# Retention attention inside a projection stream: attention in chunk halves on 64x64 quarters of the PE array, with the state in SBUF and the transposes on the DMA engines

## The chip, the cores and the metric

The kernel runs on one core of one Trainium2 chip. The metric is the device time in microseconds (us) of one execution; lower is better. Most executions of one kernel agree closely, but some run with part of their time at a lower TensorE clock. Each execution therefore carries a state (fast or slow) and a mean granted clock, and only fast runs enter a comparison. A time of 219 us here belongs to a profiled span that is about 1.7 us shorter, because the span starts at the first instruction; times are compared with times and spans with spans.

Engine names: PE is TensorE's matmuls, DVE is VectorE, ACT is ScalarE, POOL is GpSimd, SP is SyncE. SP only moves data here: it issues loads, stores and DMA transposes, in order.

## The reference

Linear attention with a decay per head feeds a two-layer projection network. Inputs and outputs are float32; the kernel may use bf16 inside.

```python
B, H, S, D = 4, 8, 768, 64
gamma = 1.0 - 2.0 ** (-5.0 - np.arange(H))
for t in range(S):                       # state is [B, H, 64, 64]
    state = gamma * state + outer(k[:, :, t], v[:, :, t])
    y[:, :, t] = (q[:, :, t] @ state) / sqrt(D)
x = y.transpose(0, 2, 1, 3).reshape(B * S, H * D)      # 3072 x 512
h = x @ w_in                             # 512 -> 2048
out = (h * cos(h)) @ w_out               # 2048 -> 512
```

## The kernel before

Tokens are taken in chunks of 128. A *pair* `p` is one chunk of two batches; there are twelve, 0 to 5 for the first two batches and 6 to 11 for the other two. Two pairs make a *group* of 512 tokens, and there are six groups. Attention of a pair has four steps on PE: transposes of q and k (`t`; on PE for pairs 0 to 5, by DMA from pair 6 on), scores (`a`), outputs from the state and from the masked scores (`y`), and the state update. The projections are `unit_f` (w_in, four matmuls of 512 columns) and `unit_o` (w_out, likewise).

```python
PT = 6                                    # from this pair on, transposes by DMA
...
def stage_t_dma(p):                       # SP issues it
    n = p % NB
    for w, src in enumerate((qs[n], ks[n])):
        nc.sync.dma_start_transpose(
            out=qkt[n][:, w].rearrange("p b a t -> p (b a) t"),
            in_=src.rearrange("p b h d -> p (b h d)"))
...
def stage_a(p):                           # scores: 64 rows x 128 columns of the array
    ...
    nc.tensor.matmul(ap[j][:, a, :], lhsT=kt(n, b, a)[po : po + 64, :],
                     rhs=qt(n, b, a)[po : po + 64, :], tile_position=(po, 0))
...
def stage_yb(p, b):                       # outputs: 128 rows x 64 columns
    ...
    nc.tensor.matmul(yp[ts(j, 64), a, :], lhsT=stb[p % 2][:, b, a, ts(j, 64)],
                     rhs=qt(n, b, a), start=True, stop=False, skip_group_check=True)
    ...
    nc.tensor.matmul(yp[ts(j, 64), a, :], lhsT=vs[n][:, b, 2 * a + j, :],
                     rhs=am[p % 2][b][j][:, a, :], start=(c == 0), stop=True,
                     skip_group_check=True)
...
def stage_s(p, copy_st):                  # the state accumulates in a PSUM bank
    ...
    nc.tensor.matmul(st_ps[ts(j, 64), b, a, :], lhsT=ks[n][:, b, h, :],
                     rhs=vs[n][:, b, h, :], start=(c == 0 and b == 0 and a == 0),
                     stop=True, skip_group_check=True)
```

The main loop spreads the attention steps between the projections. Pairs 4 and 5 run while only the output projection of group 0 is there to cover them; pairs 6 to 11 run two to a group inside three groups that have both projections.

```python
steps = {1: "t", 2: "a", 3: "m", 6: "y"}
plan = {g: [(8 * hf + r, 2 * (g + 1) + hf, w) for hf in range(2) for r, w in steps.items()]
        for g in range(2, NG - 1)}
plan[1] = [(4, 4, "t"), (5, 4, "a"), (6, 4, "m"), (9, 4, "y"),
           (9, 5, "t"), (10, 5, "a"), (11, 5, "m"), (14, 5, "y")]
for g in range(1, NG + 1):
    for s in range(16):
        if 1 < g < NG:
            unit_f(g, s)
        unit_o(g - 1, *divmod(s, 4))
        # then whatever plan[g] has at s; at "m": stage_t_dma(p + 1);
        # at "y": SP loads q0, q1, v0 of pair p + 3, POOL's queue the other three
```

## Time and profile before

| kernel before | |
|---|---|
| time, at first | 223.2 us, median of 3 runs (219.04 to 355.21) |
| time, with the runs beside the changed kernel | 221.41 us, median of 4 runs |
| most common fast time at full clock, all batches | 219.6 us |
| profiled span | 218.3 us, clock 1.0 |
| start, until the first output matmul of group 0 | 58.1 us |
| stage of pairs 4 and 5 | 20.5 us |
| three groups with pairs 6 to 11 | 94.4 us |
| rest, projections only | 45.3 us |

The page of the profile: busy time of an engine with its share of the span and its instructions; then PE's busy share and PE's clock, in tenths, for 40 equal slices of the span; then the chain of waits (the work that ended last, followed back) by engine.

```profile
PE 206.5 (95%) x1725; PEld 114.0 (52%) x1725; DVE 113.2 (52%) x183; ACT 118.4 (54%) x187; POOL 99.0 (45%) x113
...
PE   7986999989999999999999999999999999999993
...
PEclk9999999999999999999999999999999999999999
...
PE 80%; POOL 9%; DVE 4%; ACT 4%; issue 2%; DVEq 0%; POOLq 0%; ACTq 0%
```

PE is the limit after the first tenth of the span, and its clock is full throughout. The same by stages. A row holds start and end of the stage; its length and PE's busy time; then PE's weight loads, DVE, ACT and POOL; at the end PE's clock, the DMA engines' busy share and GB/s.

```profile
0.00:58.09 58.09, 50.82 (x589) 38.65 (x590) 40.12 (x72) 39.21 (x62) 54.40 (x67) 1.00 1.00 238
58.09:78.61 20.52, 19.76 (x210) 10.77 (x208) 7.73 (x12) 11.56 (x19) 20.47 (x22) 1.00 0.84 233
78.61:172.97 94.36, 94.36 (x737) 45.86 (x736) 53.18 (x81) 51.58 (x82) 24.15 (x26) 1.00 0.56 125
172.97:218.30 45.33, 41.61 (x193) 18.70 (x191) 12.19 (x18) 16.08 (x26) 0.00 (x0) 1.00 0.14 53
```

In the three groups PE is never idle, so what attention takes from PE there is paid in full. In the stage of pairs 4 and 5 the DMA engines are 84% busy, against 56% in the groups; that will matter.

PE's timeline shows what one attention pair costs there. Columns: start, duration, engine and line, tiles, shapes, count.

```profile
82.93 1.03 PE L305 MATMUL bank_69<-w_out_sb,gt_137 128*128 128x512 bf16 x4
83.89 0.23 PE L202 MATMUL bank_68<-qkt_121 64*128 64x128 bf16 x1
...
105.89 1.03 PE L305 MATMUL bank_65<-w_out_sb,gt_137 128*128 128x512 bf16 x4
...
107.76 0.42 PE L250 MATMUL st_ps<-vs_119,ks_116 128*64 128x64 bf16 x16
```

Matmuls of 512 columns start 0.216 us apart. The distance from the last of them before an attention step to the first after it, less 0.216, is what the step costs: 0.65 us for scores and 1.36 us for outputs and state update, together 2.0 us a pair. In each, 0.1 us at the start and 0.13 to 0.15 us at the end have no matmul starting. The Trainium skill, "TensorEngine Tiling (Array Packing)", Key Properties, says that a change of tiling mode drains TensorE; these gaps agree with it. SP's timeline, where the name of the tile tells loads (`qf`, `vf`) from transposes (`qkt`):

```profile
75.38 1.49 SPq L183 DMA_TRANSPOSE qkt_121<-qs_112  x1
76.93 1.90 SPq L183 DMA_TRANSPOSE qkt_121<-ks_115  x1
78.93 0.53 SPq L110 DMA_DIRECT2D qf_0_84<-in_q_dram  x1
...
80.17 1.64 SPq L110 DMA_DIRECT2D vf_0_104<-in_v_dram  x1
```

A DMA keeps SP standing for 0.5 to 1.9 us here. Nothing on PE waits for SP itself in this kernel, only for what it has moved.

### The profile page before, as it was taken

How to read it: one execution, taken by the hardware profiler on the slowest of the kernel's cores; microseconds unless marked ns; L12 is line 12 of the kernel's file. 1: busy time of each engine (PE TensorE's matmuls, PEld its weight loads, DVE VectorE, ACT ScalarE, POOL GpSimd, SP SyncE). 2: the span in 40 equal slices, each digit the busy share in tenths (PEclk: the TensorE clock that was granted, in tenths of full speed). 3: DMA queues.
4: the chain of work that ended last, by engine and by line, in shares of the span. 5: the costliest groups of instructions: out<-in, count | busy, mean ns of one | idle time of the engine just before them, and what ended most of it. 6: DMA issues, size and time to landing. Idle time of an engine off the chain costs nothing.

```text
span 218.3 us, 4318 instructions
## 1 busy us (share of the span) xinstructions
PE 206.5 (95%) x1725; PEld 114.0 (52%) x1725; DVE 113.2 (52%) x183; ACT 118.4 (54%) x187; POOL 99.0 (45%) x113
## 2 busy tenths in 40 slices
PE   7986999989999999999999999999999999999993
PEld 2554877968756454544544544544544544444441
DVE  4486496795714516557448537547647244433000
ACT  7365857848854656556456555555534634444120
POOL 7999999959999984729042070000000000000000
PEclk9999999999999999999999999999999999999999
DMA  6999999999476999792991942613511011110212
GB/s 156 324 161 235 264 282 236 203 305 332 116 241 164 291 223 290 182 296 54 182 250 55 158 127 82 66 48 99 51 48 51 0 48 48 51 48 2 96 62 82
DMA packets 44084, 32.78 MB, mean 150 GB/s; under 512 B 32800, under 2 KB 37664, under 8 KB 44064
## 3 DMA queue, kind: packets, MB, share of 16 engines
q0 software_dynamic: 9072, 18.35, 33.4%
q1 hardware_dynamic: 34848, 14.03, 27.6%
q8 instruction: 13, 0.21, 0.4%
q10 hardware_dynamic: 144, 0.13, 0.2%
q14 instruction: 7, 0.06, 0.1%
HBM read 27.26 MB, written 6.29 MB: 154 GB/s over the span
## 4 chain that ended last, share of the span: by engine, by line
PE 80%; POOL 9%; DVE 4%; ACT 4%; issue 2%; DVEq 0%; POOLq 0%; ACTq 0%
PE bank_65 L305 10%; PE bank_63 L281 9%; PE bank_67 L305 8%; PE bank_68 L305 6%; PE bank_66 L305 6%; PE bank_64 L281 5%; PE bank_69 L281 4%; PE bank_69 L305 4%; PE bank_66 L281 4%; PE bank_67 L281 3%; PE bank_63 L292 2%; PE bank_64 L292 2%; PE bank_63 L305 2%; PE bank_64 L305 2%; POOL qs_113 L151 1%
## 5 line engine op out<-in xcount | busy, mean ns | idle before, releaser
L281 PEld LDWEIGHTS <-w_in_sb 128*128 128x128 bf16 x256 | 24.1, 98 | 28.3
L305 PEld LDWEIGHTS <-gt_137 128*128 128x128 bf16 x192 | 18.8, 98 | 22.7
L305 PEld LDWEIGHTS <-gt_136 128*128 128x128 bf16 x192 | 18.5, 98 | 21.6
L292 PEld LDWEIGHTS <-w_in_sb 128*128 128x128 bf16 x256 | 24.6, 98 | 4.0 <-issue 0.9
L305 PE MATMUL bank_67<-w_out_sb,gt_136 128*128 128x512 bf16 x64 | 16.3, 379 | 0.0
L305 PE MATMUL bank_65<-w_out_sb,gt_136 128*128 128x512 bf16 x64 | 16.1, 379 | 0.0
L281 PE MATMUL bank_63<-xt_134,w_in_sb 128*128 128x512 bf16 x48 | 12.4, 380 | 0.0
L305 PE MATMUL bank_66<-w_out_sb,gt_137 128*128 128x512 bf16 x48 | 11.8, 379 | 0.0
L305 PE MATMUL bank_68<-w_out_sb,gt_137 128*128 128x512 bf16 x48 | 11.8, 379 | 0.0
L263 ACT ACTIVATE cosb_140<-bank_63,halfpi 128x512 bf16<-128x512 f32 x10 | 6.9, 688 | 7.3 <-PE bank_63 L281 6.4
L327 PE MATMUL bank_63<-gt_137 128*128 128x512 bf16 x29 | 9.1, 470 | 1.3 <-DVE gt_137 L130 1.3
L263 ACT ACTIVATE cosb_139<-bank_63,halfpi 128x512 bf16<-128x512 f32 x9 | 6.2, 688 | 7.5 <-PE bank_63 L281 6.5
L263 ACT ACTIVATE cosb_138<-bank_63,halfpi 128x512 bf16<-128x512 f32 x8 | 5.5, 688 | 7.7 <-PE bank_63 L281 7.5
L281 PE MATMUL bank_63<-xt_135,w_in_sb 128*128 128x512 bf16 x36 | 9.3, 380 | 0.0
L281 PE MATMUL bank_64<-xt_134,w_in_sb 128*128 128x512 bf16 x32 | 8.2, 380 | 0.0
L305 PE MATMUL bank_69<-w_out_sb,gt_137 128*128 128x512 bf16 x32 | 8.2, 379 | 0.0
L305 PE MATMUL bank_65<-w_out_sb,gt_137 128*128 128x512 bf16 x32 | 8.2, 379 | 0.0
L255 DVE CAST stb_133<-st_ps 64x512 bf16<-64x512 f32 x8 | 5.5, 689 | 5.0 <-PE st_ps L250 4.8
L312 DVE COPY ob_111<-bank_68 128x256 f32<-128x256 f32 x1 | 0.4, 425 | 13.3 <-PE bank_68 L305 13.3
L263 ACT ACTIVATE cosb_140<-bank_64,halfpi 128x512 bf16<-128x512 f32 x7 | 4.8, 688 | 4.6 <-PE bank_64 L281 3.0
L281 PE MATMUL bank_69<-xt_135,w_in_sb 128*128 128x512 bf16 x28 | 7.2, 379 | 0.0
L281 PE MATMUL bank_66<-xt_135,w_in_sb 128*128 128x512 bf16 x28 | 7.2, 379 | 0.0
(399 smaller groups left out, 501.4 us busy)
## 6 DMA issues: line engine op xcount, KB each, us to landing
w_out_sb<-in_moe_w_out_dram POOLq DMA_DIRECT2D x4, 512.0 KB, 9.9
w_in_sb<-in_moe_w_in_dram POOLq DMA_DIRECT2D x3, 512.0 KB, 7.5
out_dram<-ob_108 SPq DMA_DIRECT2D x6, 256.0 KB, 2.2
out_dram<-ob_109 SPq DMA_DIRECT2D x6, 256.0 KB, 2.0
out_dram<-ob_110 SPq DMA_DIRECT2D x6, 256.0 KB, 2.1
out_dram<-ob_111 SPq DMA_DIRECT2D x5, 256.0 KB, 2.0
kf_1_89<-in_k_dram POOLq DMA_DIRECT2D x3, 256.0 KB, 5.0
vf_1_99<-in_v_dram POOLq DMA_DIRECT2D x3, 256.0 KB, 5.1
```

What stands on the lines that cost most here:

```text
L151: eng.tensor_tensor(out=qs[p % NB][:, b], in0=qf[p % PRE][b], in1=bc(gq, p % NC), op=ALU.mult)
L255: copy_st(out=stb[(p + 1) % 2][ts(j, 64), :, :, ts(j, 64)], in_=st_ps[ts(j, 64)])
L263: nc.scalar.activation(out=cb, in_=bank, func=AF.Sin, bias=halfpi)
L281: nc.tensor.matmul(bank, lhsT=w_in_sb[:, i, ts(f, 128)], rhs=xt[g % 2][:, i, :], start=(i == 0), stop=(i == KIN - 1))
L292: nc.tensor.matmul(bank[:, ts(e, 256)], lhsT=w_in_sb[:, i, ts(f + e, 128)], rhs=xt[g % 2][:, i, ts(hf, 256)], start=(i == 0 and e == 0), s ...
L305: nc.tensor.matmul(bank, lhsT=gt[g % 2][:, f, ts(j, 128)], rhs=w_out_sb[:, f, :], start=(f == 0), stop=(f == KOUT - 1))
L312: nc.vector.tensor_copy(out=o[:, ts(0, 256)], in_=bank[:, ts(0, 256)])
L327: nc.tensor.matmul(spare, lhsT=zero[:, :128], rhs=zero, start=True, stop=True, skip_group_check=True)
```

## The change

The intent is to use PE better in attention. From pair 4 on, a chunk is handled as two halves of 64 tokens. Each matmul then needs only a 64x64 quarter of the array, so that four can run at once. Scores across the two halves are not needed: the first half goes through the state. Scores, outputs and state update use the same tiling, so all attention of a step forms one block with one change of mode. The block that finishes pair `p` also does scores and state update of pair `p + 1`. The state moves from PSUM to SBUF, DVE adds to it. Pair 5's transposes go to the DMA engines too. The number of attention matmuls of a full pair rises from 64 to 128. (The prediction's 80 counts the 16 transposes too, which PE makes only for pairs 0 to 5; its estimate doesn't rest on that number.)

Two matmuls that add into one place of PSUM may now come from different quarters, so the order of the output sums is enforced: the first output sum of a block waits for a `nop` on SP, which waits for the last score matmul. It is called *the hop* below. Where a block has nothing to overlap (the last pair), PE drains instead. The core of the diff, long cuts marked:

```diff
-    PT = 6
+    PQ = 4
+    PT = 5
...
+    def block(py=None, pa=None, pu=None):
...
+        def mm(bank, col, cols, row, lhsT, rhs):
+            ...
+            return nc.tensor.matmul(bank[half(col), cols], lhsT=lhsT, rhs=rhs, start=first,
+                                    stop=True, skip_group_check=True,
+                                    tile_position=(64 * row, 64 * col))
+        # state part of py's outputs; scores of pa (last = mm(...)); state update of pu
...
+        if py is not None:
+            n = py % NB
+            hop = None
+            if pu is None:
+                nc.tensor.drain()
+            else:
+                hop = nc.sync.nop(nofuse=True)
+                tc.add_manual_dep(hop.ins, last.ins.name, SYNC, reason="sums in order")
+            for b, a in BA:
+                for j in range(2):
+                    for u in range(2):
+                        m = mm(yb[u, b], j, ts(a, 64), u, vs[n][half(u), b, 2 * a + j, :],
+                               am[py % 2][j ^ b ^ u][half(u), b, a, :])
+                        if hop is not None:
+                            tc.add_manual_dep(m.ins, hop.ins.name, SYNC, reason="sums in order")
+                            hop = None
+        # masks and state adds on DVE, copies of outputs and state on ACT
...
-    conv_q(4, nc.gpsimd)
-    conv_k(4, True)
-    conv_v(4, nc.gpsimd)
-    load(nc.gpsimd, 6, ("q0", "q1", "k0", "k1", "v0", "v1"))
+    conv_q(4, nc.vector)
+    ...
+    conv_q(5, nc.vector)
+    conv_k(5)
+    stage_t_dma(5)
+    conv_v(5, nc.gpsimd)
...
+    plan = {g: [(5, "b", 2 * g + 2), (5, "c", 2 * g + 4),
+                (13, "b", 2 * g + 3), (13, "c", 2 * g + 5)] for g in range(2, NG - 1)}
+    plan[1] = [(2, "t", 4), (3, "a", 4), (4, "c", 6), (8, "b", 4), (9, "c", 7), (14, "b", 5)]
...
+                elif what == "c":
+                    conv_q(p, nc.vector if g == 1 else nc.gpsimd)
+                    conv_k(p)
+                    stage_t_dma(p)
+                    if p == 6:
+                        load(nc.sync, 7, ("q", "v0"))
+                        load(nc.gpsimd, 7, ("k", "v1"))
+                    conv_v(p, nc.gpsimd)
+                    if p + 2 < NP:
+                        load(nc.sync, p + 2, ("q", "v0"))
+                        load(nc.gpsimd, p + 2, ("k", "v1"))
```

Step `c` prepares a pair two ahead of the block. For pair 6, in the stage of pairs 4 and 5, it puts two transposes and four loads (pairs 7 and 8) on SP in one go, ahead of the hop of pair 4's outputs in SP's order.

## The prediction

> **What bounds the kernel.** The page has PE at 95% of a 218.3 us span, and the chain of waits is 80% PE. By stages (busy time by windows): 0 to 22.5 us start-up, waiting on POOL and loads; 22.5 to 58.2 the first four pairs; 58.2 to 78.7 output matmuls of group 0 with attention of pairs 4 and 5; 78.8 to 173.1 three groups with two attention pairs each, PE busy without a gap; then 45 us of pure projections. A group's 128 projection matmuls take 27.6 us (the group at 173.1 to 200.8), so three are 82.9 of 94.4 us: attention costs 11.5 us there, 1.9 us a pair, all of it on the critical path. In the timeline a score block opens a gap of 0.67 us in the projection stream and an output-and-state block one of 1.38 us, about 0.1 us of each at both ends without a matmul. This fits the Trainium skill, "TensorEngine Tiling", Key Properties: a change of tiling mode drains the engine.
>
> **What the quarters should cost.** A full pair becomes 128 matmuls of 64x64x64 instead of 80. Before, state matmuls (64 columns, two column halves) start in pairs 3 to 4 ns apart, a pair every 32 ns: streaming limits, not issue. If four quarters run together at that rate (the same page: 64x64 is four independent tiles that load and multiply in parallel), a block is 32 x 32 ns = 1.0 us plus one mode change of 0.2 us plus 0.1 to 0.2 us for the ordering wait: about 1.3 us against 2.05. Estimate for the three groups, with the smaller blocks of pairs 6, 10 and 11: 8.1 us instead of 11.5, so -3.4 us.
>
> **Group 0's outputs (20.5 us before: 13.8 of matmuls).** Removed: one pair's PE transposes (0.9 us) and one pair's wait on the ScalarE copies (about 0.7). Cheaper attention. Without new waits 18.3 us: -2.2.
>
> **The new wait.** The output sums of a block wait for a semaphore passed through SP, which is in order and also issues DMA. Before the first such hop stand both transposes of pair 6, loads of pairs 7 and 8, and a store. On SP's timeline a transpose takes 1.3 to 1.6 us to issue (up to 4.1), three loads 1.9 to 3.9 us. The transposes start only after DVE has done masks, state sums and the conversion of pair 6 (about 4 us after pair 4's scores). I reckon SP there 3 to 7 us after PE; less for the second hop. Later hops have 13 us of slack. I put +4.5 us on it. The start gets +0.3 us of POOL masks.
>
> **Off the path:** DVE gives pair 4 and 5 conversions 2.4 us, ScalarE gets state copies; both are near half busy, and eight banks cover the lag. POOL loses conversions.
>
> **Sum:** 219.97 (profiled run) - 3.4 - 2.2 + 4.5 + 0.3 = 219.2, called **219 us**, 8 in 10 within **213 to 226**. Faster by over 2%: 0.27; within 2%: 0.50; slower: 0.23.
>
> **Right or wrong in the profile.** Quarter matmuls in fours every 32 ns, and PE busy in the three groups for about 91 us instead of 94.4: the rate. A PE idle of some microseconds at pair 4's output sums, released by SP, while SP issues loads: the hop. Stage after the first four pairs longer than 20.5 us: the hop outweighs the saving there.
>
> **What would make it wrong.** Weight loads of the two row halves not overlapping: 64 ns per four, a block near 2.2 us, no gain, 222 to 225. SP ahead of PE after all: 214 to 215. SP also late in the later groups: each late hop adds its full wait. Row halves waiting for each other at a shared PSUM bank: slower quarters.

## The result, and the profile after

| | before | after |
|---|---|---|
| time, median of 4 runs | 221.41 us | 233.59 us (232.47 to 234.5) |
| ratio of fast runs | | 1.065, 95% interval 1.056 to 1.074 |
| profiled span | 218.3 us | 231.4 us |
| clock in the profiled run | 1.0 | 0.953 |
| start | 58.1 | 59.4 |
| stage of pairs 4 and 5 | 20.5 | 34.5 |
| three groups | 94.4 | 92.0 |
| rest | 45.3 | 45.5 |

A ratio in this document is the mean time of one kernel's fast runs over the mean of the other's fast runs of the same rounds, so it is not quite the ratio of the medians. The change is slower by over 2%, outside the predicted range of 213 to 226 us. Of the 13.1 us by which the span grew, 14.0 lie in the stage of pairs 4 and 5, the start gives 1.3, the rest 0.2, and the three groups give 2.3 back.

The page after, the same lines as before:

```profile
PE 207.2 (90%) x2221; PEld 112.4 (49%) x2221; DVE 111.7 (48%) x197; ACT 122.3 (53%) x214; POOL 83.1 (36%) x93
...
PE   7885999989992493999999999999999999999993
...
PEclk9999799999998578599999999999999999999999
...
PE 74%; POOL 8%; SPq 7%; ACT 4%; DVE 4%; issue 2%; DVEq 0%; POOLq 0%; ACTq 0%
```

SP's sequencer (SPq) is in the chain with 7%, where it had no share. PE has holes in the thirteenth, fourteenth and sixteenth slice, and its clock falls from the thirteenth to the seventeenth. By stages:

```profile
0.00:59.36 59.36, 51.35 (x590) 38.69 (x591) 40.32 (x76) 38.71 (x64) 51.53 (x63) 0.97 1.04 253
59.36:93.88 34.52, 22.37 (x387) 11.15 (x385) 14.06 (x28) 11.82 (x25) 15.33 (x16) 0.80 0.93 215
93.88:185.91 92.03, 91.92 (x1056) 43.89 (x1056) 45.09 (x77) 55.67 (x103) 16.23 (x16) 0.98 0.41 93
185.91:231.40 45.49, 41.60 (x193) 18.67 (x191) 12.19 (x18) 16.07 (x26) 0.00 (x0) 0.99 0.14 52
```

In the second row PE is busy for 22.4 of 34.5 us. What PE waited for there, as total, times and longest in us:

```profile
PE bank_69 L306 <- SPq L341: 6.6, 1, 6.6
PE bank_67 L306 <- SPq L341: 3.7, 1, 3.7
...
PE bank_69 L306 <- DMA qkt_108<-ks_102: 1.2, 1, 1.2
```

Line 341 is the hop. Two of the hops were waited for, those of pairs 4 and 5, with 10.3 us together. The third wait is for pair 5's transposes, which go by DMA now. SP's timeline tells why the first hop was late:

```profile
68.40 1.25 SPq L205 DMA_TRANSPOSE qkt_106<-qs_97  x1
69.70 1.73 SPq L205 DMA_TRANSPOSE qkt_106<-ks_100  x1
71.54 0.52 SPq L120 DMA_DIRECT2D qf_80<-in_q_dram  x1
72.16 2.28 SPq L120 DMA_DIRECT2D vf_90<-in_v_dram  x1
74.55 0.76 SPq L120 DMA_DIRECT2D qf_81<-in_q_dram  x1
75.42 1.93 SPq L120 DMA_DIRECT2D vf_91<-in_v_dram  x1
77.44 0.91 SPq L438 DMA_DIRECT2D out_dram<-ob_94  x1
```

And PE's timeline at the same time:

```profile
71.42 0.42 PE L306 MATMUL st_ps<-vs_105,ks_102 64*64 64x64 bf16 x16
78.45 0.26 PE L306 MATMUL bank_69<-am_0_0_109,vs_104 64*64 64x64 bf16 x1 [6.61 <-SPq L341]
```

PE had done everything that could be done without the hop at 71.84. SP then stood at four loads and a store until 78.35, and PE went on 0.1 us later, with pair 4's output sums. A `nop` that takes no time waited 6.5 us for its turn.

The clock falls with it. Busy times of the stretches around the two waits, columns as above with the clock third from the end:

```profile
69.90:73.30 3.40, 0.74 (x56) 0.58 (x48) 0.00 (x0) 0.00 (x0) 0.00 (x0) 1.00 1.34 237
73.30:76.70 3.40, 0.00 (x0) 0.00 (x0) 0.00 (x0) 0.00 (x0) 0.00 (x0) 0.50 1.14 257
76.70:80.10 3.40, 1.65 (x35) 0.94 (x36) 1.18 (x4) 0.38 (x2) 1.04 (x2) 0.50 1.22 300
80.10:83.50 3.40, 3.40 (x9) 1.22 (x8) 3.00 (x4) 2.53 (x6) 3.38 (x4) 0.50 0.23 37
83.50:87.00 3.50, 3.50 (x73) 1.66 (x74) 0.00 (x0) 0.58 (x1) 1.68 (x2) 0.99 1.03 247
87.00:90.40 3.40, 0.52 (x60) 0.41 (x47) 0.00 (x0) 0.00 (x0) 0.00 (x0) 0.99 0.99 215
90.40:93.80 3.40, 2.46 (x36) 1.10 (x37) 2.04 (x6) 1.27 (x5) 2.01 (x3) 0.50 0.81 214
```

For 10.2 us (73.3 to 83.5) and again for 6.8 us (90.4 to 97.2) PE had half its clock: matmuls of 512 columns started 0.43 us apart, not 0.216. The Trainium skill, "TensorE: Matmul & The Clock Gate", Part 1: The HAM clock gate, has a free-running window of 3413 ns, half rate after an idle window and full rate after a busy one. The stretches of half clock inside the spans of all the profiles were 3.4, 6.8 or 10.2 us long, one, two or three such windows, which agrees. But the windows that led to the two falls here were not quite idle: PE was busy for 0.74 us in the first and for 0.52 us in the second. And windows that were busy for 1.65 and 2.46 us did not bring the clock back, while a full one did. The same count over the windows inside all seventeen profiles: those with 1.4 us of matmuls or less were all followed by half rate, those with 1.8 us or more never; between the two both happened (1.76 us in e2 was followed by it, 1.62 us in e14 was not). Half rate stayed after windows with up to 2.87 us (e5) and ended after those with 2.92 us (e13) or more. So PE need not stand for a whole window: in e4 a wait of 2.3 us was enough. Ends of matmuls are modelled in a profile, so these limits are rough.

In the three groups the change does what it was made for. A block there:

```profile
135.16 1.03 PE L425 MATMUL bank_69<-w_out_sb,gt_122 128*128 128x512 bf16 x4
136.12 0.22 PE L306 MATMUL bank_64<-qkt_108,stb_118 64*64 64x64 bf16 x2
...
137.35 0.82 PE L401 MATMUL bank_68<-xt_121,w_in_sb 128*128 128x512 bf16 x3
```

Four quarter matmuls start every 30 to 36 ns. A block costs the projection stream 1.19 to 1.33 us (1.02 for the last) where a pair cost 2.0. So tiles of one mode do run side by side, as "TensorEngine Tiling (Array Packing)", Key Properties, says of loads and matmuls of different tiles. The gain is the difference between 94.4 and 92.0 us, and the half clock until 97.2 hides a part of it.

### The profile page after: what moved, and what is told of

The parts are those of the page before. It is cut to its first block, busy times and chain, and to the rows that moved or that the text cites. A ratio compares the mean times of both kernels' runs of the same rounds, so it can differ in the third digit from the quotient of the medians.

```text
span 231.4 us, 5291 instructions
## 1 busy us (share of the span) xinstructions
PE 207.2 (90%) x2221; PEld 112.4 (49%) x2221; DVE 111.7 (48%) x197; ACT 122.3 (53%) x214; POOL 83.1 (36%) x93
## 4 chain that ended last, share of the span: by engine, by line
PE 74%; POOL 8%; SPq 7%; ACT 4%; DVE 4%; issue 2%; DVEq 0%; POOLq 0%; ACTq 0%
PE bank_67 L425 9%; PE bank_68 L425 5%; PE st_ps L425 4%; PE bank_63 L425 4%; PE bank_64 L425 4%; PE bank_68 L401 4%; PE bank_69 L401 4%; SPq L120 4%; PE bank_66 L401 3%; PE bank_65 L401 3%; PE st_ps L401 3%; PE bank_65 L425 3%; PE bank_69 L425 3%; PE bank_64 L401 3%; SPq L205 2%; PE bank_63 L401 2%
## 5 line engine op out<-in xcount | busy, mean ns | idle before, releaser
L401 PEld LDWEIGHTS <-w_in_sb 128*128 128x128 bf16 x256 | 24.8, 99 | 30.4 <-issue 2.1
L425 PEld LDWEIGHTS <-gt_122 128*128 128x128 bf16 x192 | 19.2, 101 | 23.6 <-issue 3.5
L425 PEld LDWEIGHTS <-gt_123 128*128 128x128 bf16 x192 | 19.0, 99 | 23.3 <-issue 1.1
L412 PEld LDWEIGHTS <-w_in_sb 128*128 128x128 bf16 x256 | 25.3, 101 | 5.6 <-issue 1.6
L425 PE MATMUL bank_67<-w_out_sb,gt_123 128*128 128x512 bf16 x48 | 12.7, 400 | 0.0
L425 PE MATMUL bank_67<-w_out_sb,gt_122 128*128 128x512 bf16 x48 | 11.8, 380 | 0.0
L425 PE MATMUL st_ps<-w_out_sb,gt_123 128*128 128x512 bf16 x48 | 11.8, 380 | 0.0
L425 PE MATMUL bank_68<-w_out_sb,gt_122 128*128 128x512 bf16 x32 | 9.8, 463 | 0.0
L425 PE MATMUL bank_66<-w_out_sb,gt_122 128*128 128x512 bf16 x32 | 8.8, 411 | 0.0
L425 PE MATMUL bank_63<-w_out_sb,gt_122 128*128 128x512 bf16 x32 | 8.2, 380 | 0.0
L425 PE MATMUL bank_69<-w_out_sb,gt_122 128*128 128x512 bf16 x32 | 8.2, 380 | 0.0
L425 PE MATMUL bank_65<-w_out_sb,gt_123 128*128 128x512 bf16 x32 | 7.7, 380 | 0.0
L425 PE MATMUL bank_64<-w_out_sb,gt_123 128*128 128x512 bf16 x32 | 7.7, 380 | 0.0
L401 PE MATMUL bank_69<-xt_120,w_in_sb 128*128 128x512 bf16 x28 | 7.2, 380 | 0.0
L181 POOL TENSOR_TENSOR vs_104<-vf_90,gk 128x512 bf16<-128x512 f32 x2 | 2.0, 1037 | 12.5 <-PE bank_69 L306 12.5
L401 PE MATMUL bank_68<-xt_121,w_in_sb 128*128 128x512 bf16 x24 | 6.2, 380 | 0.0
L401 PE MATMUL bank_65<-xt_121,w_in_sb 128*128 128x512 bf16 x24 | 6.2, 379 | 0.0
L361 ACT CAST xt_120<-bank_69 128x256 bf16<-128x256 f32 x2 | 0.8, 375 | 10.0 <-DVE am_0_0_113 L354 10.0
L375 ACT CAST stb_117<-stf 128x512 bf16<-128x512 f32 x8 | 4.9, 618 | 1.9 <-DVE stf L372 1.7
## 6 DMA issues: line engine op xcount, KB each, us to landing
w_out_sb<-in_moe_w_out_dram POOLq DMA_DIRECT2D x4, 512.0 KB, 10.2
```

The lines of the kernel that those rows point to most:

```text
L181: eng.tensor_tensor(out=vs[p % NB][:, b], in0=vf[p % PRE][:, b], in1=bc(gk, p % NC), op=ALU.mult)
L361: nc.scalar.copy(out=xt[(py // 2) % 2].rearrange("p a (h b u t) -> p h b u a t", h=2, b=2, u=2)[:, py % 2, b, u], in_=yb[u, b][:, :256].re ...
L375: nc.scalar.copy(out=stb[pu % 2][:, u], in_=stf[:, u])
L401: nc.tensor.matmul(bank, lhsT=w_in_sb[:, i, ts(f, 128)], rhs=xt[g % 2][:, i, :], start=(i == 0), stop=(i == KIN - 1))
L412: nc.tensor.matmul(bank[:, ts(e, 256)], lhsT=w_in_sb[:, i, ts(f + e, 128)], rhs=xt[g % 2][:, i, ts(hf, 256)], start=(i == 0 and e == 0), s ...
L425: nc.tensor.matmul(bank, lhsT=gt[g % 2][:, f, ts(j, 128)], rhs=w_out_sb[:, f, :], start=(f == 0), stop=(f == KOUT - 1))
```

## The experiments

Fifteen kernels ran, all with correct results. In the texts, letters stand for the theories as held then. A is that the loss is the hop's place behind SP's work; B, the rival, that the wait only hides that transposes, conversions or masks of pairs 4 to 6 come too late, whoever carries the hop; C, that the 64x64 matmuls themselves bring the clock down; D, which came later, that what is left after the hop is pair 5's transposes by DMA in a stage with full DMA engines; E, that pair 7's loads come late in the new order and hold up whatever queue carries the hop; F, the last, that the loads in the stage come too close together and that spreading them is what remains. In e1, e2, e3, e5, e6, e8, e9, e11, e13 and e15 the time came out above the forecast of the theory tested, even where the wait in question went as expected. Stage figures are us from the profile of one run each; when that run was slow it is said.

| run | start | stage of pairs 4, 5 | three groups | ratio to before, fast runs, 95% |
|---|---|---|---|---|
| before | 58.1 | 20.5 | 94.4 | 1 |
| after | 59.4 | 34.5 | 92.0 | 1.065 (1.056 to 1.074) |
| e1, drain | 57.8 | 26.6 | 91.6 | 1.009 (1.001 to 1.017) |
| e2, loads behind | 58.3 | 26.8 | 92.0 | 1.023 (1.015 to 1.031) |
| e3, wait filled | 58.8 | 35.5 | 90.4 | 1.053 (1.043 to 1.062) |
| e4, hop on POOL | 60.0 | 24.2 (slow run) | 90.4 | 0.995 (0.984 to 1.005) |
| e5, and pair 5 on PE | 58.1 | 23.8 | 92.4 | 1.004 (0.998 to 1.011) |
| e6, quarters from pair 6 | 58.0 | 20.5 (slow run) | 97.5 | 0.991 (0.985 to 0.998) |
| e7, before with DMA transposes of 5 | 57.2 | 19.1 | 94.9 | 0.999 (0.988 to 1.009) |
| e8, e5 with pair 7 early | 57.7 | 24.8 | 90.5 | 0.998 (0.990 to 1.007) |
| e9, e6 respaced | 57.8 | 20.5 | 91.9 | 0.989 (0.981 to 0.998) |
| e10, e9 with DMA transposes of 5 | 57.8 | 19.6 | 92.0 | |
| e11, e10 one unit earlier | 60.5 | 19.1 | 92.7 | 0.994 (0.991 to 0.997) |
| e12, e11 with hop on SP | 59.4 | 19.7 | 92.4 | 0.993 (0.991 to 0.995) |
| e13, e4 with pair 8 later | 59.1 | 23.1 | 92.2 | 0.994 (0.987 to 1.001) |
| e14, e13 with pair 5 on PE | 58.1 | 23.0 | 90.5 | |
| e15, e13 with pair 7 earlier | 61.6 | 20.2 | 90.5 | 0.991 (0.988 to 0.994) |

### Is it the hop through SP?

**e1_drain.** Every block drains PE; no hop.

```diff
-            if pu is None:
+            if True:
                 nc.tensor.drain()
```

> Every ordering hop through SP becomes a drain of PE itself; nothing else changes. Theory A (the hop stands in SP's queue behind transposes, loads and a store; the PE idle then halves the granted clock): the waits of 6.6 and 3.7 us and the half-clock stretches after them (about 5.3 us lost) go, seven drains cost 0.1 to 0.2 us each; about 218.5 us, 216.5 to 220.5. Rival B (the wait only hides that transposes, conversions or masks of pairs 4 to 6 come too late): PE stops at almost the same place for one of those, time stays above 226. Rival C (the 64x64 matmuls themselves lower the granted clock): the waits go but half-clock stretches stay, about 223.

Measured: 222.45 us (221.41 to 223.34). Most of the loss went with the hop, so SP's queue is its main cause. The expected 218.5 was missed, though: the stage still took 26.6 us, and a new wait stood in it.

```profile
PE bank L306 <- DMA qkt<-ks: 3.0, 1, 3.0
```

The transposes of pair 5 came 3.0 us late, with two windows at half clock after them (70.9 to 77.7). The rival was partly right. In the groups a block with a drain costs 1.45 to 1.58 us, so that the hop, when its engine is free, is about 0.25 us cheaper.

**e2_loads_behind.** SP's loads are issued behind the block, so that only transposes and a store stand before the hop.

```diff
                     if p == 6:
-                        load(nc.sync, 7, ("q", "v0"))
                         load(nc.gpsimd, 7, ("k", "v1"))
...
-                        load(nc.sync, p + 2, ("q", "v0"))
                         load(nc.gpsimd, p + 2, ("k", "v1"))
...
                     block(py=p if what != "a" else None, pa=nxt, pu=nxt)
+                    for i in {4: (7, 8), 5: (9,), 6: (10,), 7: (11,)}.get(p, ()) if what == "b" else ():
+                        load(nc.sync, i, ("q", "v0"))
```

> The hop stays on SP, but SP's loads of q and v are issued after the hop of the next block instead of before it; transposes and the store stay ahead. Theory A with the loads as the main part: SP is free at about the moment PE comes (its transposes ended at 71.4 us, PE came at 71.7), so the first wait falls from 6.6 us to under 1.5, time within 1.5 us of e1, 217 to 221. If the transposes are the main part: first wait stays above 3 us, time above 225. Rival B: above 226.

Measured: 225.6 us (224.27 to 226.89). PE's waits for SP fell from 10.3 us to 2.0. Over half of the change's surplus in the stage (7.7 of 14.0 us) is gone although the hop stays on SP. It is mostly the loads ahead of it that made it dear. The time is still above the expected 217 to 221: the transposes of pair 5 came 1.5 us late, and two stretches of half clock remained (71.3 to 78.1 and 84.9 to 88.3).

**e3_fill_wait.** Matmuls whose results nobody reads fill PE's wait for the two hops. This takes the clock's fall away and leaves the wait.

```diff
+    FILL = {4: 29, 5: 20}
...
+            if py in FILL:
+                sp = banks.free_list[0]
+                for _ in range(FILL[py]):
+                    nc.tensor.matmul(sp, lhsT=w_in_sb[:, 0, :128], rhs=w_in_sb[:, 0, :512],
+                                     start=True, stop=True, skip_group_check=True)
```

> The changed kernel with its hops, but 29 dummy matmuls of 512 columns (6.3 us) before the first wait and 20 (4.3 us) before the second, into a bank that is free; they change no result. The waits stay as long, only PE is busy in them. Theory A: the granted clock stays full after them, 3.5 to 5.5 us come back, 228 to 230.5 us. Rival C (the clock falls because of the 64x64 matmuls, or at that time anyway): half-clock stretches stay, 232 us or more.

Measured: 232.65 us (230.93 to 235.6), about one per cent less than the changed kernel. PE's timeline shows the second filled wait and the sums behind the hop:

```profile
85.80 4.49 PE L343 MATMUL bank<-w_in_sb 128*128 128x512 bf16 x19
91.70 0.44 PE L308 MATMUL bank<-am,vs 64*64 64x64 bf16 x32 [1.41 <-SPq L348]
```

The clock was full from the first fill to the end of the groups, and yet the first sums of pair 5 started at 91.70 against 91.18. Between the two hops SP sets the pace: 12.58 us here (79.12 to 91.70), 12.73 in the changed kernel (78.45 to 91.18). There the half clock costs 0.15 us at most. From the second hop to the end of the groups it took 93.0 us here and 94.7 with half clock, so the half clock behind the second hop is worth 1.7 us. The wait is the cause, the clock an addition. Theory C falls too: with the same 64x64 matmuls the clock stayed full. Less came back than the 3.5 to 5.5 us expected.

**e4_hop_on_pool.** The hop goes through POOL. POOL issues loads too, but in this run the last of those ahead of the first hop was done at 66.3 us, before PE came.

```diff
-                hop = nc.sync.nop(nofuse=True)
+                hop = nc.gpsimd.nop(nofuse=True)
```

> The same hop, through POOL's queue instead of SP's. POOL stands idle from about 66.5 us on, waiting for this very block. Theory A: the first hop passes at once, as fast as e1 within 2 us (217 to 221); a later hop may meet POOL waiting for a load, then 1 to 4 us more. If a hop as such (two semaphores) costs much more than a drain: 2 us or more above e1 with no single long wait.

Measured: 220.96 us (218.49 to 223.25); its two fast runs took 218.49 and 220.08. One word moves the kernel from 6.5% slower to level with before. In the profile, of a slow run:

```profile
59.97:84.18 24.21, 19.41 (x383) 10.78 (x385) 14.02 (x28) 11.82 (x25) 9.99 (x10) 0.93 1.11 206
84.18:174.60 90.42, 89.68 (x1044) 43.62 (x1056) 45.09 (x77) 55.51 (x103) 20.20 (x20) 1.00 0.47 119
```

By these rows the hop's place was worth 10.3 us of the stage and 1.6 of the groups. The stage is still above the 20.5 us of before, and PE still waited 2.3 us for the transposes of pair 5, with 3.4 us of half clock after it.

### What is left of the stage's surplus?

**e5_pool_pe_transpose5.** As e4, with pair 5 transposed on PE again.

```diff
-    PT = 5
+    PT = 6
...
     conv_k(5)
-    stage_t_dma(5)
     conv_v(5, nc.gpsimd)
...
-    plan[1] = [(2, "t", 4), (3, "a", 4), (4, "c", 6), (8, "b", 4), (9, "c", 7), (14, "b", 5)]
+    plan[1] = [(2, "t", 4), (3, "a", 4), (4, "c", 6), (5, "t", 5), (8, "b", 4), (9, "c", 7), (14, "b", 5)]
...
-                    stage_t(p, False)
+                    stage_t(p, p == 5)
```

> e4 (hop on POOL) with pair 5 transposed on PE again, as in the kernel before; its two DMA transposes are gone. In e1 and e4 PE waited 3.0 and 2.3 us for their landing, with a half-clock stretch just then (3.4 to 6.8 us long). Theory D (what is left of the loss after the hop is the transposes of pair 5 in a stage in which the DMA engines are full): the wait and the half-clock stretch go, PE does 0.9 us more; 215.5 to 218, faster than before. Rival (loads of pairs 6 to 8 or DVE would hold PE there anyway): another wait of 2 us or more in pair 4's block, 219 or more.

Measured: 221.01 us (220.36 to 222.42), not faster than e4. The wait for the transposes is gone and another has its place: the hop, on POOL now, stood behind the conversion of v of pair 7, which waited for its load.

```profile
PE bank L306 <- POOLq L341: 2.5, 1, 2.5
```

**e6_quarters_from_pair6.** Pairs 4 and 5 as before the change, quarters from pair 6 on (`PQ = 6`, `PT = 6`), hop on POOL. The first half of `plan[1]` and the loads there are those of the kernel before.

```diff
-    PQ = 4
+    PQ = 6
...
+    plan[1] = [(4, "t", 4), (5, "A", 4), (6, "m", 4), (9, "y", 4),
+               (9, "t", 5), (10, "A", 5), (11, "m", 5), (14, "y", 5), (15, "c", 7)]
+    plan[2].insert(0, (2, "a", 6))
```

> The first six pairs and their schedule as in the kernel before; quarters and state in SBUF only from the seventh pair on (a new batch pair, so no state is handed over), hop on POOL. If the quarters save what the later groups showed (about 4 us over three groups) and the loss lies in the stage of pairs 4 and 5: 215 to 217 us, output matmuls of group 0 take 20.5 to 21.5 us again. If quarters cost something elsewhere: 218.5 or more.

Measured: 220.44 us (218.12 to 223.25), ratio 0.991. The stage is back at 20.5 us, in a profile of a slow run, but the groups took 97.5: PE waited 4.6 us in two waits for the DMA transposes of pairs that come too soon after.

**e7_before_transpose5_by_dma.** The kernel before with `PT = 5` and nothing else. If DMA transposes of pair 5 were dear in themselves, this kernel would show it.

```diff
-    PT = 6
+    PT = 5
```

> The kernel before with one part of the change alone: pair 5 transposed by DMA instead of PE. PE saves 0.9 us of transposes and the 0.4 us wait on the copies. Theory D: the DMA engines are full there, PE waits 1 to 3 us for the landing at pair 5's scores; 219.5 to 222, not faster than before. Rival (DMA transposes as such are harmless there): 218.5 or less.

Measured: 219.83 us (218.44 to 221.68), ratio 0.999. Its two runs at full clock, 218.44 and 218.53, are about 1 us below the common 219.6 of the kernel before, and the stage took 19.1 us. The longest wait for those transposes was 0.5 us. So the theory that the DMA transposes alone cost it falls: they save PE's work and come in time, where SP's queue and the DMA engines are not full of loads.

**e8_load7_early.** As e5, with SP's loads of pair 7 moved ahead of the stage.

```diff
     conv_k(5)
+    load(nc.sync, 7, ("q", "v0"))
     conv_v(5, nc.gpsimd)
...
                     if p == 6:
-                        load(nc.sync, 7, ("q", "v0"))
                         load(nc.gpsimd, 7, ("k", "v1"))
```

> e5 with one more move: SP issues the loads of q and v of pair 7 before pair 4's stage, not behind the transposes of pair 6. In e5 PE waited 2.5 us for the hop on POOL, which stood behind the conversion of v of pair 7, which had to wait for its load; a half-clock stretch followed. Theory E (the changed order brings pair 7's loads late, so that whatever queue carries the hop waits for them): the 2.5 us wait goes and with it the half-clock stretch; 216.5 to 219. Rival (the DMA engines have no room in that stage, an earlier load only delays another): a wait of 2 us or more elsewhere, 220 or more.

Measured: 220.47 us (219.18 to 220.96), no difference to be told. POOL's hop is on time, and PE waits for the transposes of pair 6 instead, for 3.1 us. That wait left the clock full: it fell across two windows, and PE was busy for 1.79 us in each. Removing the wait that ends last only uncovers the next one, as long as the same traffic is squeezed into the same stage.

**e13_load8_later.** As e4; the loads of pair 8, which nobody needs for 20 us, are issued behind the block of pair 5.

```diff
-                    if p + 2 < NP:
+                    if p != 6 and p + 2 < NP:
                         load(nc.sync, p + 2, ("q", "v0"))
...
                     block(py=p if what != "a" else None, pa=nxt, pu=nxt)
+                    if what == "b" and p == 5:
+                        load(nc.sync, 8, ("q", "v0"))
+                        load(nc.gpsimd, 8, ("k", "v1"))
```

> e4 with one move: the loads of pair 8 are issued after pair 5's block, not before pair 4's, so that in the stage of pairs 4 and 5 the DMA engines carry one pair's loads and the transposes, not two pairs' loads. Theory F (the rest of the loss in that stage, 24.2 us in e4 against 20.5, is DMA traffic packed into too short a time, behind which the transposes of pair 5 and then the load of pair 7 come late): the 2.3 us wait falls below 1 us, the stage takes 20 to 22 us, 215.5 to 218 in all. Rival (the transposes themselves, slow to issue and land, not the loads beside them): the wait stays over 2 us, 219 or more.

Measured: 219.62 us (218.72 to 221.65). The wait for the transposes of pair 5 is gone (2.3 us in e4), in a kernel in which SP had the same work ahead of them. What had held them up, then, were loads of pair 8 that POOL's queue had issued; one profile of each kernel shows it. The Trainium skill, "Trainium Kernel Development and Optimization", Key Constraints, says that DMAs from the queues of SP, ACT and POOL run on the same 16 DMA engines and interleave; these runs agree. What remains is the hop on POOL behind v of pair 7, whose load SP had only issued at 72.5:

```profile
PE bank L306 <- POOLq L341: 2.7, 1, 2.7
```

**e14_load8_later_pe5.** As e13, with pair 5 transposed on PE; the edit is that of e5.

> e13 with pair 5 transposed on PE as in e5. Theory F: the wait of 2.5 us that e5 had for the load of pair 7 goes too; stage 20 to 21.5 us, 215.5 to 217.5. If e13 still waits for transposes and this one does not, the transposes are the late part, not the loads. If both keep waits over 2 us, neither is the cause.

Measured: one fast run of 218.86 us and three slow ones (222.23 to 224.43). The profile of the fast run has a stage of 23.0 us and a wait of 1.8 us for the same hop. It tells that pair 5's transposes are no longer what matters.

**e15_loads_spread.** As e13, with SP's loads of pair 7 issued before the stage.

```diff
     conv_k(5)
+    load(nc.sync, 7, ("q", "v0"))
     stage_t_dma(5)
...
                     if p == 6:
-                        load(nc.sync, 7, ("q", "v0"))
                         load(nc.gpsimd, 7, ("k", "v1"))
```

> e13 and the move of e8 together: pair 8's loads after pair 5's block, and SP's loads of pair 7 before pair 5's transposes instead of behind pair 6's. In e13 the wait for pair 5's transposes was gone and a wait of 2.7 us was left, the hop on POOL behind the conversion of pair 7, whose load SP had issued at 72.5 us. Theory F: that wait goes too, stage of pairs 4 and 5 20 to 21.5 us, no half-clock stretch after it, 215.5 to 217.5 us. Rival (any order leaves PE waiting there): a wait of 1.5 us or more, 218.5 or more.

Measured: 218.83 us, median of 6 runs (217.02 to 221.7), ratio 0.991. No output sum waits for a hop in its profile, and no block for a DMA transpose:

```profile
61.56:81.71 20.15, 18.00 (x382) 10.01 (x384) 13.20 (x28) 11.72 (x25) 11.19 (x11) 1.00 0.93 180
81.71:172.20 90.49, 89.75 (x1044) 43.53 (x1056) 45.10 (x77) 55.63 (x103) 20.26 (x21) 1.00 0.51 128
```

Stage 20.2 us and groups 90.5 us are the best pair of all runs. The start took 61.6 us here, with half clock from 20.4 to 27.2; so this profile doesn't show the kernel at its best. The waits for hops and DMA transposes that the change had brought are gone, with the hop off SP and the loads spread, and all the rest of the change is left in. One new wait is left, which the kernel before doesn't have: at the end of the stage the first projection of group 2 waits for ACT's copies of pair 5's outputs. No run tried to remove it with pairs 4 and 5 in quarters.

```profile
PE bank L401 <- ACT xt L361: 1.2, 1, 1.2
```

### Can the rest be made to pay?

**e9_pair6_respaced.** As e6, with the block of pair 6 and the preparation of pair 8 two units later, and the loads of pair 9, which e6 issues right behind pair 7's transposes, six units later (a unit is one of the 16 steps `s` of a group in the main loop).

```diff
-    plan[2].insert(0, (2, "a", 6))
+    plan[2] = [(2, "a", 6), (5, "l", 9), (7, "b", 6), (7, "c", 8), (13, "b", 7), (13, "c", 9)]
...
-                    if p + 2 < NP:
+                    if p > 7 and p + 2 < NP:
...
+                elif what == "l":
+                    load(nc.sync, p, ("q", "v0"))
+                    load(nc.gpsimd, p, ("k", "v1"))
```

> e6 with more room: the loads of pair 9 are issued 6 units later, and the first full block comes 2 units later, so that the DMA transposes of pairs 6 and 7 have landed when PE comes. In e6 PE waited 2.4 and 2.2 us for these. Waits gone: about 4.6 us less plus the half-clock stretch, 213 to 216, against about 219.5 of the kernel before. If the three groups are not faster by some 4 us after that, the quarters' gain was not what the gaps showed: 217 or more.

Measured: 218.35 us (217.45 to 218.98), ratio 0.989 (0.981 to 0.998). The groups took 91.9 us where e6 took 97.5, and no wait for transposes is longer than 0.5 us. Against the 90.4 to 90.5 us of the best runs, 0.8 us more is the block of pair 6's scores and state update, which lies in the groups here and in the changed kernel at the end of the stage before.

**e10_and_transpose5_by_dma.** As e9, with `PT = 5`, the transposes of pair 5 by DMA.

```diff
-    PT = 6
+    PT = 5
...
-                    if p == 5:
-                        stage_t_dma(6)
+                    stage_t_dma(p + 1)
```

> e9 with pair 5 transposed by DMA, as in e7, where that alone took about 1 us off at full clock. 0.5 to 1.5 us faster than e9 if the two add up; slower than e9 if the DMA engines then delay the transposes of pair 6 or 7.

Measured: two fast runs, 216.46 and 217.21 us, and two slow ones, 222.93 and 223.75. The profile of the first has the shortest span of all, 214.8 us, at full clock.

**e11_best.** As e10, with the block of pair 6 one unit earlier.

```diff
-    plan[2] = [(2, "a", 6), (5, "l", 9), (7, "b", 6), (7, "c", 8), (13, "b", 7), (13, "c", 9)]
+    plan[2] = [(2, "a", 6), (5, "l", 9), (6, "b", 6), (6, "c", 8), (13, "b", 7), (13, "c", 9)]
```

> e10 with the first full quarter block and the conversion of pair 8 one unit earlier, so that pair 8's transposes have landed at the next block (a wait of 0.5 us there in e9 and e10). 0.3 to 0.7 us less than e10 at the same clock: 215.5 to 217 in full-clock runs, 1.0 to 2.2% faster than the kernel before over the fast runs.

Measured: 218.68 us, median of 6 runs (217.72 to 222.82), ratio 0.994. A miss: the transposes of a pair came 1.3 us too late, and the kernel is no better than e9.

**e12_best_hop_on_sp.** As e11, with the hop on SP again. If an SP hop is dear in itself, this must be much slower; if only what stands ahead of it counts, it must be level.

```diff
-                hop = nc.gpsimd.nop(nofuse=True)
+                hop = nc.sync.nop(nofuse=True)
```

> e11 with the hop back on SP. Theory A says that the hop costs only what stands before it in SP's queue: here SP has the transposes of pair 7 and the loads of pair 9 behind it by about 90 us and PE comes at about 91.5, so no wait over 0.7 us and a time within 0.5% of e11. Rival (a hop through SP is slow in itself): each of the five later blocks 0.3 us or more longer, 1.5 us or more over e11.

Measured: 218.41 us, median of 6 runs (217.06 to 218.74), ratio 0.993, level with e11. PE waited for SP once:

```profile
PE bank L301 <- SPq L336: 0.3, 1, 0.3
```

So there is nothing slow about a semaphore that passes through SP. The blocks in this kernel all have projections of both kinds around them, and SP is through with what stands ahead of a hop, or nearly so, when PE comes.

## Why the prediction was wrong

**The step that failed** is the size of the new wait: "I put +4.5 us on it." Together the hop through SP cost 11.9 us, by the profiles of the changed kernel and of e4: 10.3 in the stage of pairs 4 and 5 (34.5 against 24.2) and 1.6 in the groups (92.0 against 90.4). The profile of e4 is of a slow run; fast runs of the two kernels (mean 219.3 of e4's two, median 233.59 of the changed kernel's, measured at different times) are 14.3 us apart. So 12 to 14 us is its size.

The mechanism was the predicted one. PE's idle time at pair 4's output sums, released by SP while SP issued loads, was named in advance, and the first wait, 6.6 us, lies within the "3 to 7 us" of the prediction. Three things were missing in the sum:

- The second hop was put down as "less". Less it was, but its 3.7 us had no place in a sum of 4.5: transposes of pair 7, loads and a store were ahead of it in the same way.
- The fall of the clock wasn't foreseen at all. The second wait's half clock is worth 1.7 us (e3); the first one's was hidden by SP's pace.
- By the prediction's own figures, "3 to 7" and then "less", 4.5 us is hardly more than the first hop alone.

The hop is not the whole miss. The profiled run of the changed kernel took 233.1 us, 13.9 more than the 219.2 of the sum. With e4 (a slow run) for the kernel without the SP hop, 7.4 of them are the hop (11.9 against 4.5), 5.9 the stage without it (+3.7 against -2.2), 1.0 the start and 0.2 the rest; the groups gave 0.6 more than predicted.

**The other terms:**

- *"Without new waits 18.3 us: -2.2."* This step failed as well, because the hop was not the only new wait. Once it was out of the way the stage took 24.2 us in e4 (slow run), with 2.3 us of waiting for pair 5's DMA transposes, 3.4 us of half clock after it and 1.3 us of waiting for ACT's copies of pair 5's outputs at its end, and 23.1 in e13. With loads spread it took 20.2 in e15, a gain of 0.3 us on before; 1.2 us of its distance to 18.3 is the wait for these copies. In profiles the loads' order is worth up to 4.1 us (24.2 to 20.2). In the times of fast runs it is worth much less: 219.3 (e4) against 218.2 (mean of e15's fast runs, 219.37, 218.28, 218.12, 217.02). Which of the two is the truer size stays open, because e4's profile was slow and e15's start was.
- *"SP ahead of PE after all: 214 to 215."* That alternative was too hopeful. With the hop off SP the kernel took 218.49 and 220.08 in its fast runs (e4), and with the loads spread too 217.02 at best (e15).
- *Quarters in the groups, -3.4 us.* Right. With a full clock and no waits the groups took 90.4 to 90.5 us (e3, e4, e8, e14, e15), 3.9 to 4.0 less than before. Part of it is moved, not saved: pair 6's scores and state update are done in the stage now, and cost 0.80 us where they stand as a block of their own (e9, e12). In the changed kernel's own profile it is 2.3, because the half clock reaches to 97.2 us.
- *"About 1.3 us against 2.05"* for a block. Right: 1.19 to 1.33 against 2.0.
- *Start, +0.3 us.* It was 1.3 us in the profile. That run had half clock from 22.1 to 25.5. POOL's masks are not to blame, since PE began its projections slightly earlier than before. In the ten profiles without such a stretch the start took 57.2 to 58.3 us, in the seven with one or two 58.8 to 61.6. Fast runs of the kernel before also show a mean clock of 0.992 now and then, so this isn't shown to belong to the change.

**Where the expected gain went:** it was given, 3.9 us of it in the groups. The stage of pairs 4 and 5 took it back more than threefold, for the most part through a queue that orders a `nop` behind DMAs. With that mended (e15), the kernel beats the one before by 0.9% (ratio 0.991, 0.988 to 0.994), within 2% as are e9 and e12. By the profile of e15 the groups and the stage give 4.2 us; about 2 appear in the times (0.9% of 220). The start took 1 to 3 us more in some profiles of the changed kernels, with half clock there, and why that is so wasn't settled.

## What to carry to other kernels

A dependency that is passed through an engine costs that engine's whole backlog, and an issued DMA is backlog even if the engine is "idle" by its busy time. Before such a hop is put into a stage, sum what the carrier issues ahead of it in that stage, for each hop, and count a possible fall of the clock if PE would stand for about half of a 3.4 us window or more (falls came here after windows with up to 1.76 us of matmuls). When a wait is removed and another of nearly the same length takes its place, look at the traffic that both depend on (here the loads of two pairs in one short stage), and spread that.

## What the Trainium skill lacked or had wrong

- "DMA: Bandwidth & Descriptors" doesn't say how long an issuing engine stands at one DMA when the DMA engines are loaded. In the crowded stage of the changed kernel SP stood 0.5 to 2.3 us at a load and 1.24 to 3.35 us at a transpose; in e8 one load took it 6.8 us.
- "TensorEngine Tiling (Array Packing)" says that a change of mode drains the engine, but not what it costs. Here it was about 0.10 us on the way in and 0.13 us on the way out. No page has a measured rate for 64x64 tiles with 64 columns; here four such matmuls started every 30 to 36 ns.
- No page compares a drain of PE with a wait that is passed through another engine. Here the drain cost a block about 0.25 us more (1.45 to 1.58 against 1.19 to 1.33 us), if the other engine was free.
- "TensorE: Matmul & The Clock Gate", Part 1: The HAM clock gate, speaks of an idle window before the rate falls. Here windows with up to 1.76 us of matmuls in 3.4 us were followed by half rate as well (e2). How much work a window needs to keep or to regain the full rate is not said; here 1.8 us kept it in every case, 2.87 us did not regain it (e5), and 2.92 us did (e13).
